# Seven products for eight in the up product of a fused retention and tanh-shrink kernel

## The chip, the cores and the metric

The kernel runs on one core of one Trainium2 chip. The metric is the device time of one execution in microseconds. Five engines work side by side, each in the order of its own queue, and wait for one another by semaphores: TensorE (PE in the profile, its weight loads PEld), VectorE (DVE), ScalarE (ACT), GpSimd (POOL) and SyncE (SP, which starts transfers). TensorE writes its results into PSUM[...]; GpSimd does not reach PSUM in this kernel.

## The reference

```python
# q, k, v: (4, 8, 768, 64)
for t in range(768):
    state = gamma * state + outer(k[t], v[t])      # per batch and head
    y[t] = scale * q[t] @ state
x = y.transpose(0, 2, 1, 3).reshape(3072, 512)
h = x @ w_in                                       # 512 -> 2048
g = h - tanh(h)
out = g @ w_out                                    # 2048 -> 512
```

All of it is in float32; `w_in` and `w_out` arrive as 64-bit floats and are converted on the chip.

## The kernel before

The tokens are cut into 24 chunks of 128 for the attention and into 12 half blocks `n` of 256 tokens (`TH`) for the two large products. The hidden dimension is cut into 8 pairs `m2` of two 128-wide tiles. A *step* is one half block with one pair, so there are 96 steps, numbered `s` from 0; half blocks 4 to 11 have eight steps each, 32 to 95.

The first steps are issued in an order written out by hand, with the conversion of the weights in between (`keep_busy` there puts filler products of 128 columns on zeros into TensorE's queue). From step 8 on one loop issues everything; each engine keeps the order of the program, since the schedule is manual. Per step the loop does this:

- `up` (line 420): 8 products, 128x128 weights of `w_in` against 256 tokens, into one PSUM bank `h` (two such banks in turn; the left and the right half hold the two tiles of the pair). Each float32 product is two instructions of TensorE, so a step has 16.
- `shrink_begin` (lines 429, 430): ScalarE takes the square `u` and the tanh `th` of the bank.
- `shrink_factors` (437 to 439): ScalarE makes `q0`, `q1` and `large` from `u`.
- `shrink_multiply` (445 to 448): VectorE makes h - tanh(h) and multiplies two factors of a polynomial onto `h`, in PSUM.
- `shrink_end` (454 to 459): the last factor, the product with `u` into `g` in SBUF, and a predicated copy that puts h - tanh(h) where |h| is not small.
- `fast_sums` (545 to 548): four sums of quarters of `g` by GpSimd, each 128x128.
- `downs(LAG)`: the down product of the step two before (`LAG` = 2).

The down product of half blocks 5 to 11 (`FAST` = 5) is already in seven products for eight, in Winograd's form of Strassen's scheme: `fast_down` (line 581) makes seven products of 256 columns (14 instructions) from sums of `g` and of `w_out`, accumulated over the eight steps of a half block in seven halves of PSUM banks. `fast_end` joins them at the end of a half block: one ScalarE copy and seven VectorE sums (lines 590 to 602), with the two output transfers on SP. `fast_weights` (line 536) makes the sums of `w_out` once, on GpSimd. For half blocks before that, `down` (line 468) makes four products of 512 columns (8 instructions).

The attention of the last chunks runs in the same loop, at odd steps up to 45: `keep_x`, `products`, `mask`, `state`, `turn_by_dma` (ScalarE copies of 16-bit words and a transfer that transposes them) and `outputs`; GpSimd scales q and v of a later chunk (`scale`, line 240) at the end of the step before.

Of the kernel before, what the change touches and what calls it, by code (L numbers as in the profile page):

```python
# [9 lines left out]
F32 = mybir.dt.float32  # L10
# [3 lines left out]
AF = mybir.ActivationFunctionType  # L14
ALU = mybir.AluOpType

P = 128
# [15 lines left out]
def kernel(  # L33
# [7 lines left out]
    tables: bass.AP,  # L41
    out: bass.AP,
):

# [11 lines left out]
    nc = tc.nc  # L58
# [10 lines left out]
    NB = NCH // BLK  # L69
    BANK = 512  # L70
    TH = 2 * P
    LAG = 2
# [3 lines left out]
    stage = ctx.enter_context(tc.tile_pool(name="stage", bufs=2))  # L76
# [20 lines left out]
    at = [0]  # L97
# [22 lines left out]
    NW = 2 * NM  # L120
# [289 lines left out]
    def work(tag, bufs):  # L410
        return tmp.tile([P, BANK], F32, tag=tag, name=tag, bufs=bufs)

    def up(n, m2, i):

        if i == 0:
            hps[n, m2] = bank("h", f"h_{n}_{m2}")
        hp = hps[n, m2][:, ts(i, TH)]
        keep_busy(hp[:, :P])
        for c in range(NC):
            nc.tensor.matmul(hp, w1[:, c, ts(2 * m2 + i, P)], xT[n // 2][:, c, ts(n % 2, TH)],  # L420
                             start=(i == 0 and c == 0), stop=(c == NC - 1),
                             skip_group_check=True)
# [3 lines left out]
    def shrink_begin(n, m2):  # L426
        hp = hps[n, m2]
        u, th = (work(x, 2) for x in ("u", "th"))
        nc.scalar.activation(u, hp, AF.Square)  # L429
        nc.scalar.activation(th, hp, AF.Tanh)  # L430
        shrinking[n, m2] = [u, th]

    def shrink_factors(n, m2):
        u = shrinking[n, m2][0]
        large = work("large", 2)
        q0, q1 = (work(x, 1) for x in ("q0", "q1"))
        nc.scalar.activation(q0, u, AF.Square, bias=bias0)  # L437
        nc.scalar.activation(q1, u, AF.Square, bias=bias1, scale=math.sqrt(A))  # L438
        nc.scalar.activation(large, u, AF.Relu, bias=bias_m)  # L439
        shrinking[n, m2] += [q0, q1, large]  # L440

    def shrink_multiply(n, m2):
        hp = hps[n, m2]
        u, th, q0 = shrinking[n, m2][:3]
        nc.vector.tensor_tensor(th, hp, th, op=ALU.subtract)  # L445
        nc.vector.scalar_tensor_tensor(hp, in0=u, scalar=R, in1=hp, op0=ALU.subtract,  # L446
                                       op1=ALU.mult, reverse0=True)
        nc.vector.scalar_tensor_tensor(hp, in0=q0, scalar=C0, in1=hp, op0=ALU.add,  # L448
                                       op1=ALU.mult)

    def shrink_end(n, m2):
        hp = hps.pop((n, m2))
        u, th, _, q1, large = shrinking.pop((n, m2))
        nc.vector.scalar_tensor_tensor(hp, in0=q1, scalar=A * C1, in1=hp, op0=ALU.add,  # L454
                                       op1=ALU.mult)
        g = gp.tile([P, 2, TH], F32, tag="g", name=f"g_{n}_{m2}")
        flat = g.rearrange("p i t -> p (i t)")
        nc.vector.tensor_tensor(flat, hp, u, op=ALU.mult)  # L458
        nc.vector.copy_predicated(flat, large.bitcast(I32), th)  # L459
        gT[n, m2] = g  # L460
# [25 lines left out]
    def rows_of(n):  # L486

        return out[ds(n * TH, TH)].rearrange("(p two) c -> p two c", two=2)
# [19 lines left out]

    FAST = 5
    PAIRS = NM // 2  # L510
    room = []
    t_of = {}

    def quarter(i, c, at):
        return w2[:, i::2, ts(c, TH)][:, ds(2 * at, 2)]

    def fast_weights(k, at):

        if not room:
            for _ in range(3):  # L520
                raw = stage.tile([P, 2, 2, TH], F32, tag="raw", name="fast_raw", bufs=3)
                room.extend(raw[:, i] for i in range(2))
            for tag in ("head", "low", "power"):
                room.extend(stage.tile([P, 2, TH], F32, tag=tag, name=f"fast_{tag}")
                            for _ in range(2))
        if k == 3 and at == 0:
            late = xp.tile([P, 4, 2, TH], F32, tag="xT", name="fast_x")
            room.extend(late[:, i] for i in range(4))
        t = t_of[k, at] = room[PAIRS // 2 * k + at]
        a, b = (  # L530
            (quarter(0, 1, at), quarter(0, 0, at)),
            (quarter(1, 1, at), t_of.get((0, at))),
            (quarter(1, 1, at), quarter(0, 1, at)),
            (t_of.get((1, at)), quarter(1, 0, at)),
        )[k]
        nc.gpsimd.tensor_tensor(t, a, b, op=ALU.subtract)

    fast_g = {}

# [28 lines left out]
        right = {2: 1, 7: 1, 4: 1, 6: n % 2}  # L568
        accs[n] = {k: b[:, ts(right.get(k, 0), TH)] for k, b in acc.items()}

    def fast_down(n, m2, first, last):
        if first:
            fast_banks(n)
        left = fast_g.pop((n, m2))
        for k in (1, 2, 4, 6, 7, 5, 3):
            right = (
                w2[:, 2 * m2, :TH], w2[:, 2 * m2 + 1, :TH], w2[:, 2 * m2 + 1, TH:],
                *(t_of[x, m2 // 2][:, m2 % 2] for x in (3, 0, 1, 2)),
            )[k - 1]

            nc.tensor.matmul(accs[n][k], left[k - 1], right, start=first and k in (1, 6, 7, 4),  # L581
                             stop=last, skip_group_check=True)

    def fast_end(n):
        acc = accs.pop(n)
        o = op.tile([P, 2, DM], F32, tag="sum", name=f"sum_{n}")
        c11, c12, c21, c22 = (o[:, j, ts(c, TH)] for j in range(2) for c in range(2))
        some = [mid.tile([P, 2, TH], F32, tag="a", name=f"fast_{n}") for _ in range(2)]
        p1, v_, x_, w_ = (t[:, i] for t in some for i in range(2))
        nc.scalar.copy(out=p1, in_=acc[1])  # L590
        add, sub = ALU.add, ALU.subtract
        for dst, k, b, how in (
            (c11, 2, p1, add), (v_, 6, p1, add), (w_, 7, v_, add), (c22, 5, w_, add),
            (x_, 5, v_, add), (c21, 4, w_, sub), (c12, 3, x_, add),
        ):
            if how is sub:
                nc.vector.tensor_tensor(dst, b, acc[k], op=sub)
            else:
                nc.vector.tensor_tensor(dst, acc[k], b, op=add)
            if dst is c21:  # L600
                nc.sync.dma_start(out=rows_of(n)[:, 1], in_=o[:, 1])
        nc.sync.dma_start(out=rows_of(n)[:, 0], in_=o[:, 0])

    waiting = []

    def part(j, n, m2, first, last):
        down(n, m2, j, first, last)
        if last:
            add_up(n, m2, j)

    def downs(lag):
        while len(waiting) > lag:
            tile_ = waiting.pop(0)
            if tile_[0] >= FAST:
                fast_down(*tile_)
                if tile_[3]:
                    fast_end(tile_[0])
                continue
            for j in range(2):
                part(j, *tile_)  # L620

# [52 lines left out]


    FIRST = 8
    LAST_WEIGHTS = NW - 6
    with_chunk = {BEGUN + 2 * i + 1: FIRST - 3 + i for i in range(NCH - FIRST + 3)}  # L680
    with_weights = {BEGUN: [12, 13]}
    for i in range(14, NW):
        with_weights[i - 5] = [i]
    fast_parts = [(k, at) for at in range(PAIRS // 2) for k in range(3)]
    fast_parts += [(3, at) for at in range(PAIRS // 2)]

    for s in range(BEGUN, len(steps)):
        n, m2, first, last = steps[s]
        ci = with_chunk.get(s)
        if ci is not None:  # L690
            if ci >= FIRST:
                outputs_rest(ci)
                keep_x(ci)
            if FIRST <= ci + 2 < NCH:
                products(ci + 2)
                mask(ci + 2)
                state(ci + 2)
            load_chunk(ci + 4)
            if ci + 3 < NCH:
                turn_by_dma(ci + 3)  # L700
            if FIRST <= ci + 1 < NCH - 1:
                outputs(ci + 1)
                see(ci + 1)
        for i in with_weights.get(s, []):
            convert(i)
            load_weights(i + 3)
        for i in range(2):
            up(n, m2, i)
        if ci == NCH - 2:
            outputs(ci + 1)  # L710
            see(ci + 1)
        waiting.append(steps[s])
        shrink_begin(n, m2)
        shrink_factors(n, m2)
        shrink_multiply(n, m2)
        downs(LAG)
        shrink_end(n, m2)
        if n >= FAST:
            fast_sums(n, m2)
        if s + 1 in with_chunk:  # L720
            for which in range(2):
                scale(with_chunk[s + 1] + 3, which, nc.gpsimd)
        if s > LAST_WEIGHTS + 1:
            for _ in range(min(2, len(fast_parts))):
                fast_weights(*fast_parts.pop(0))
    downs(0)


def _tables(H, D, S=768):
# [51 lines left out]
```

## Time and profile before

| what | us |
|---|---|
| median of 3 runs | 733.02 (732.61 to 735.18) |
| the profiled execution | 733.69 |
| its span in the profile | 731.9 |
| busy in it: TensorE, VectorE, ScalarE, GpSimd | 717.7, 533.6, 389.7, 247.6 |
| step 32 begins about | 287.7 |
| step 95 begins its up product | 713.2 |

A line of the profile's groups gives the line of the kernel, the engine, the operation, the output and inputs by name, their shapes, and the count. A line of the order in time gives the start, the length, the engine, the line, and in brackets how long the engine had been idle and what released it. The stretches give busy time and count for each engine, in the order PE, PEld, DVE, ACT, POOL, and then the granted TensorE clock, the share of the transfers and GB/s.

### The profile page before, as it was taken

What the parts mean: (1) busy time and instruction counts of PE and PEld (TensorE: products, weight loads), DVE (VectorE), ACT (ScalarE), POOL (GpSimd) and SP (SyncE); (2) the same over time, 40 slices, a digit from 0 to 9 for tenths busy, and PEclk for the clock granted to TensorE, in tenths of its full rate; (3) what the DMA queues carried; (4) which work ended last, traced back from release to release, by engine and by line L of the source; (5) the groups of instructions that cost most, each with busy time, mean ns of one, the idle gap of its engine ahead of it and who ended that gap; (6) DMA issues with size and microseconds to landing.
All of it is one profiled execution on the core that took longest, in us unless ns stands there. A gap on an engine that the chain in (4) does not pass through costs nothing.

```text
span 731.9 us, 14885 instructions
## 1 busy us (share of the span) xinstructions
PE 717.7 (98%) x5806; PEld 566.9 (77%) x5806; DVE 533.6 (73%) x849; ACT 389.7 (53%) x749; POOL 247.6 (34%) x348
## 2 busy tenths in 40 slices
PE   8899999999999999999999999999999999999996
PEld 7686666666776676677688888888888888888885
DVE  4999988998888777765566676676766766766764
ACT  4567557766777645565445444444444444444441
POOL 0565434544554555411012222222132222222221
PEclk9999999999999999999999999999999999999998
DMA  9883428776776566444100000000000000000000
GB/s 202 211 207 84 130 69 218 173 197 171 188 192 165 110 147 165 131 106 122 36 30 1 1 29 2 1 29 1 29 1 1 30 0 1 30 0 1 30 0 30
DMA packets 125399, 59.84 MB, mean 82 GB/s; under 512 B 109840, under 2 KB 118160, under 8 KB 125328
## 3 DMA queue, kind: packets, MB, share of 16 engines
q1 hardware_dynamic: 122880, 50.34, 28.4%
q10 hardware_dynamic: 2448, 8.54, 3.1%
q8 instruction: 46, 0.75, 0.4%
q14 instruction: 25, 0.20, 0.1%
HBM read 35.80 MB, written 14.68 MB: 69 GB/s over the span
## 4 chain that ended last, share of the span: by engine, by line
PE 91%; DMA 4%; DVE 2%; POOL 1%; SPq 1%; ACT 1%; issue 0%; DVEq 0%; POOLq 0%; ACTq 0%
PE h L420 44%; PE o L468 17%; PE fast_t L581 8%; PE y L581 8%; PE fast_o L581 7%; PE y L356 3%; DMA kqT<-rows 1%; PE s L302 1%; PE s L308 1%; DMA raws<-in_moe_w_in_dram 1%; DMA k<-in_k_dram 1%; DMA q<-in_q_dram 1%; SPq L233 1%; PE kqTp L254 1%; DMA rows<-apart 1%; DVE head L189 0%
## 5 line engine op out<-in xcount | busy, mean ns | idle before, releaser
L420 PE MATMUL h<-xT,w 128*128 128x256 f32 x1536 | 349.9, 381 | 1.1 <-DVE w L203 1.1
L420 PEld LDWEIGHTS h<-xT,w 128*128 128x128 f32 x1536 | 289.7, 190 | 50.1 <-issue 10.0
L429 ACT ACTIVATE u<-h 128x512 f32<-128x512 f32 x96 | 57.3, 597 | 259.7 <-PE h L420 259.5
L445 DVE TENSOR_TENSOR th<-h,th 128x512 f32<-128x512 f32 x96 | 66.2, 689 | 132.3 <-ACT th L430 132.2
L468 PE MATMUL o<-w,g 128*128 128x512 f32 x320 | 144.2, 593 | 0.0
L545 POOL TENSOR_TENSOR s<-g 128x128 f32<-128x128 f32 x56 | 25.5, 455 | 286.7 <-DVE g L459 282.3
L468 PEld LDWEIGHTS o<-w,g 128*128 128x128 f32 x320 | 60.5, 190 | 59.5 <-issue 56.7
L459 DVE COPY_PREDICATED g<-large,th 128x512 f32<-128x512 int32 x96 | 74.3, 774 | 9.8 <-DVE g L458 0.5
L448 DVE SCALAR_TENSOR_TENSOR h<-q,h 128x512 f32<-128x512 f32 x96 | 66.8, 696 | 10.0
L199 POOL TENSOR_TENSOR low<-low,power 128x512 f32<-128x512 f32 x30 | 38.6, 1288 | 102.4 <-DVE power L191 62.8
L454 DVE SCALAR_TENSOR_TENSOR h<-q,h 128x512 f32<-128x512 f32 x96 | 66.6, 694 | 8.9 <-DVE h L448 0.9
L458 DVE TENSOR_TENSOR g<-h,u 128x512 f32<-128x512 f32 x96 | 66.4, 692 | 6.9
L437 ACT ACTIVATE q<-u,tab 128x512 f32<-128x512 f32 x96 | 69.5, 724 | 0.0
L438 ACT ACTIVATE q<-u,tab 128x512 f32<-128x512 f32 x96 | 69.1, 720 | 0.0
L439 ACT ACTIVATE large<-u,tab 128x512 f32<-128x512 f32 x96 | 68.8, 716 | 0.0
L446 DVE SCALAR_TENSOR_TENSOR h<-u,h 128x512 f32<-128x512 f32 x96 | 65.8, 685 | 0.0
L430 ACT ACTIVATE th<-h 128x512 f32<-128x512 f32 x96 | 56.8, 591 | 0.0
L240 POOL TENSOR_TENSOR q<-q,tab 128x512 f32<-128x512 f32 x22 | 24.2, 1099 | 77.2 <-DMA q<-in_q_dram 52.0
L203 POOL TENSOR_TENSOR w<-low,head 128x512 f32<-128x512 f32 x30 | 38.5, 1284 | 2.4
L240 POOL TENSOR_TENSOR v<-v,tab 128x512 f32<-128x512 f32 x22 | 28.2, 1284 | 3.3 <-DMA v<-in_v_dram 3.3
L356 PEld LDWEIGHTS y<-a,v 64*64 64x64 f32 x768 | 15.9, 134 | 14.9 <-ACT large L439 10.9
L546 POOL TENSOR_TENSOR s<-s,g 128x128 f32<-128x128 f32 x56 | 25.6, 457 | 4.4
(110 smaller groups left out, 868.7 us busy)
## 6 DMA issues: line engine op xcount, KB each, us to landing
rows<-apart ACTq DMA_DIRECT2D x16, 512.0 KB, 4.4
k<-in_k_dram SPq DMA_DIRECT2D x24, 256.0 KB, 4.7
q<-in_q_dram SPq DMA_DIRECT2D x24, 256.0 KB, 5.1
v<-in_v_dram SPq DMA_DIRECT2D x24, 256.0 KB, 5.5
raw<-in_moe_w_out_dram SPq DMA_DIRECT2D x12, 512.0 KB, 4.1
out_dram<-sum SPq DMA_DIRECT2D x24, 256.0 KB, 2.3
raw<-in_moe_w_in_dram SPq DMA_DIRECT2D x14, 256.0 KB, 4.4
raw<-in_moe_w_in_dram SPq DMA_DIRECT2D x28, 128.0 KB, 4.2
```

The lines of the kernel that those rows point to most:

```text
L420: nc.tensor.matmul(hp, w1[:, c, ts(2 * m2 + i, P)], xT[n // 2][:, c, ts(n % 2, TH)], start=(i == 0 and c == 0), stop=(c == NC - 1), skip_g ...
L437: nc.scalar.activation(q0, u, AF.Square, bias=bias0)
L438: nc.scalar.activation(q1, u, AF.Square, bias=bias1, scale=math.sqrt(A))
L439: nc.scalar.activation(large, u, AF.Relu, bias=bias_m)
L445: nc.vector.tensor_tensor(th, hp, th, op=ALU.subtract)
L446: nc.vector.scalar_tensor_tensor(hp, in0=u, scalar=R, in1=hp, op0=ALU.subtract, op1=ALU.mult, reverse0=True)
L448: nc.vector.scalar_tensor_tensor(hp, in0=q0, scalar=C0, in1=hp, op0=ALU.add, op1=ALU.mult)
L454: nc.vector.scalar_tensor_tensor(hp, in0=q1, scalar=A * C1, in1=hp, op0=ALU.add, op1=ALU.mult)
L458: nc.vector.tensor_tensor(flat, hp, u, op=ALU.mult)
L459: nc.vector.copy_predicated(flat, large.bitcast(I32), th)
L468: nc.tensor.matmul(o_p[j], gT[n, m2][:, i, ts(j, P)], w2[:, 2 * m2 + i], start=(first and i == 0), stop=(last and i == 1))
L581: nc.tensor.matmul(accs[n][k], left[k - 1], right, start=first and k in (1, 6, 7, 4), stop=last, skip_group_check=True)
```

## The change

The up product of half blocks 4 to 11 (`FAST_UP` = 4, 64 steps) is put into the seven-product form too. Left are quarters of `w_in` for the pair (each two tiles of 128 deep), right are quarters of the half block's 256 tokens, 128 columns each. A step has 14 products of 128 columns (28 instructions), all into one bank of four 128-column places:

1. `fast_up(..., (1, 5, 7, 6))` makes products 1, 5, 7 and 6 in places 0 to 3.
2. `up_take`: ScalarE copies the whole bank to SBUF (one buffer, `odd_room[0]`).
3. `up_pairs`: GpSimd makes two sums from the copy, 1 + 6 and 5 + 7 (128x256, into `odd_room[1]`).
4. `fast_up(..., (2, 3, 4))` adds products 2, 3 and 4 on top of places 0, 1 and 2.
5. `up_add`: VectorE adds the first sum to places 1 and 2 (128x256) and writes the total of the two sums to place 3 (128x128).

The sums of the operands are made by GpSimd: `up_weights` once per pair, at steps 28 to 35 (four differences or sums of 128x256), `up_tokens` once per half block (four of 128x256). `fast_weights` is now made per pair, at steps 40 to 47, in other buffers and with the same number of elements.

The order within a step changes as well. The factors of a step are split over two: the loop first ends the step before (`shrink_factors`, `shrink_end`), then does `up_pairs`, the sums for later steps, `fast_sums` of the step before, up to two of the output sums that `fast_end` now leaves for later (`end_some(2)`), the first half of the down product, the second products, `up_add`, tanh and square of `h` (tanh first), `q0`, the second half of the down product, and two factors. The last two steps have an order of their own.

```diff
     def shrink_begin(n, m2):
         hp = hps[n, m2]
         u, th = (work(x, 2) for x in ("u", "th"))
-        nc.scalar.activation(u, hp, AF.Square)
-        nc.scalar.activation(th, hp, AF.Tanh)
+        if n < FAST_UP:
+            nc.scalar.activation(u, hp, AF.Square)
+            nc.scalar.activation(th, hp, AF.Tanh)
+        else:
+            nc.scalar.activation(th, hp, AF.Tanh)
+            nc.scalar.activation(u, hp, AF.Square)
         shrinking[n, m2] = [u, th]
+
+    def shrink_factor(n, m2):
+        q0 = work("q0", 1)
+        nc.scalar.activation(q0, shrinking[n, m2][0], AF.Square, bias=bias0)
+        shrinking[n, m2].append(q0)
...
+    PLACE = {1: 0, 5: 1, 7: 2, 6: 3, 2: 0, 3: 1, 4: 2}
+
+    def fast_up(n, m2, some):
+        if 1 in some:
+            hps[n, m2] = bank("h", f"h_{n}_{m2}")
+        for k in some:
+            for c in range(2):
+                nc.tensor.matmul(hps[n, m2][:, ts(PLACE[k], P)], s_of[m2][k - 1][:, c],
+                                 x_of[n][k - 1][:, c], start=(k == 1 and c == 0), stop=(c == 1),
+                                 skip_group_check=True)
+
+    def up_take(n, m2):
+        nc.scalar.copy(out=odd_room[0], in_=hps[n, m2])
+
+    def up_pairs():
+
+        first = odd_room[0].rearrange("p (i t) -> p i t", i=4)
+        nc.gpsimd.tensor_tensor(odd_room[1], first[:, :2], first[:, 3:1:-1], op=ALU.add)
+
+    def up_add(n, m2):
+        hp = hps[n, m2].rearrange("p (i t) -> p i t", i=4)
+        u, w = (odd_room[1][:, i] for i in range(2))
+        nc.vector.tensor_tensor(hp[:, 1:3], hp[:, 1:3],
+                                u[:, None, :].to_broadcast([P, 2, P]), op=ALU.add)
+        nc.vector.tensor_tensor(hp[:, 3], u, w, op=ALU.add)
...
+    def up_weights(m2):
+
+        a11, a12, a21, a22 = (w1[:, ds(2 * c, 2), ts(2 * m2 + i, P)]
+                              for i in range(2) for c in range(2))
+        s_ = {k: next(up_room).rearrange("p (c m) -> p c m", c=2) for k in (2, 3, 4)}
+        s_[1] = a21
+        for k, x, y, how in ((3, a11, a21, ALU.subtract), (1, a21, a22, ALU.add),
+                             (2, s_[1], a11, ALU.subtract), (4, a12, s_[2], ALU.subtract)):
+            nc.gpsimd.tensor_tensor(s_[k], x, y, op=how)
+        s_of[m2] = (a11, a12, s_[4], a22, s_[1], s_[2], s_[3])
+
+    def up_tokens(n, t):
+
+        x = xT[n // 2][:, :, ts(n % 2, TH)]
+        b11, b12, b21, b22 = (x[:, ds(2 * c, 2), ts(i, P)] for c in range(2) for i in range(2))
+        t = t.rearrange("p (k c t) -> p k c t", k=4, c=2)
+        t1, t2, t3, t4 = (t[:, i] for i in range(4))
+        for dst, a, b in ((t1, b12, b11), (t2, b22, t1), (t3, b22, b12), (t4, b21, t2)):
+            nc.gpsimd.tensor_tensor(dst, a, b, op=ALU.subtract)
+        x_of[n] = (b11, b21, b22, t4, t1, t2, t3)
+
...
+    def end_some(n):
+        for _ in range(min(n, len(ending))):
+            ending.pop(0)()
...
         nc.scalar.copy(out=p1, in_=acc[1])
+        add(c11, 2, p1)
+        add(v_, 6, p1)
+        for args in ((w_, 7, v_), (c22, 5, w_), (x_, 5, v_), (c21, 4, w_, True), (c12, 3, x_)):
+            ending.append(lambda args=args: add(*args))
...
+        if fast:
+            fast_up(n, m2, (1, 5, 7, 6))
+            up_take(n, m2)
+        else:
+            for i in range(2):
+                up(n, m2, i)
         if ci == NCH - 2:
             outputs(ci + 1)
             see(ci + 1)
         waiting.append(steps[s])
-        shrink_begin(n, m2)
-        shrink_factors(n, m2)
-        shrink_multiply(n, m2)
-        downs(LAG)
-        shrink_end(n, m2)
-        if n >= FAST:
-            fast_sums(n, m2)
+        if fast:
+
+
+            final = s == len(steps) - 1
+            if final:
+                shrink_factor(*before)
+                shrink_multiply(*before)
+            if before:
+                shrink_factors(*before)
+                if final:
+                    shrink_last_factor(*before)
+                else:
+                    shrink_end(*before)
+            up_pairs()
+            for make in with_sums.get(s, []):
+                make()
+            if before and before[0] >= FAST and not final:
+                fast_sums(*before)
+            end_some(2)
+            downs(LAG, int(final))
+            fast_up(n, m2, (2, 3, 4))
+            up_add(n, m2)
+            shrink_begin(n, m2)
+            if final:
+                shrink_end(*before, begun=True)
+                fast_sums(*before)
+            if s != len(steps) - 2:
+                shrink_factor(n, m2)
+                if not final:
+                    downs(LAG, 1)
+                shrink_multiply(n, m2)
+            before = n, m2
+        else:
+            shrink_begin(n, m2)
+            shrink_factors(n, m2)
+            shrink_multiply(n, m2)
+            downs(LAG)
+            shrink_end(n, m2)
+            for make in with_sums.get(s, []):
+                make()
         if s + 1 in with_chunk:
             for which in range(2):
                 scale(with_chunk[s + 1] + 3, which, nc.gpsimd)
-        if s > LAST_WEIGHTS + 1:
-            for _ in range(min(2, len(fast_parts))):
-                fast_weights(*fast_parts.pop(0))
+    shrink_factors(*before)
+    shrink_end(*before)
+    fast_sums(*before)
     downs(0)
+    end_some(len(ending))
```

## The prediction

> **What bounds the kernel now.** I read the engine totals first, then the chain of work that ended last, then the stage that the change touches by stretches, then one step of it in order of time.
>
> ```profile
> PE 717.7 (98%) x5806; PEld 566.9 (77%) x5806; DVE 533.6 (73%) x849; ACT 389.7 (53%) x749; POOL 247.6 (34%) x348
> PE h L420 44%; PE o L468 17%; PE fast_t L581 8%; PE y L581 8%; PE fast_o L581 7%; PE y L356 3%; DMA kqT<-rows 1%; PE s L302 1%; PE s L308 1%; DMA raws<-in_moe_w_in_dram 1%; DMA k<-in_k_dram 1%; DMA q<-in_q_dram 1%; SPq L233 1%; PE kqTp L254
> ```
>
> TensorE carries the span, and the up product (L420) is 44% of the chain. The stretches (busy us and count for PE, PEld, DVE, ACT, POOL) show the last 50 steps, 389.4 to 713.2 us: no hole in TensorE, VectorE at 68%. The chain there has one period: 16 up instructions, then 14 down instructions.
>
> ```profile
> 389.40:713.20 323.80, 323.80 (x1503) 285.05 (x1502) 219.60 (x342) 147.76 (x258) 87.10 (x200) 1.00 0.03 11
> 603.29 3.45 PE h L420 x16
> 608.47 1.29 PE y L581 x6
> 609.76 3.45 PE h L420 x16
> ```
>
> So a step takes 609.76 - 603.29 = 6.47 us: 16 x 0.2157 = 3.45 up and 14 x 0.2157 = 3.02 down. One step of the other engines, in order of time:
>
> ```profile
> 561.45 0.60 ACT L429 ACTIVATE u<-h 128x512 f32<-128x512 f32 x1 [3.56 <-PE h L420]
> 561.95 0.59 ACT L430 ACTIVATE th<-h 128x512 f32<-128x512 f32 x1
> 562.57 0.69 DVE L445 TENSOR_TENSOR th<-h,th 128x512 f32<-128x512 f32 x1 [1.94 <-ACT th L430]
> 563.18 0.69 DVE L446 SCALAR_TENSOR_TENSOR h<-u,h 128x512 f32<-128x512 f32 x1
> 563.97 0.70 DVE L448 SCALAR_TENSOR_TENSOR h<-q,h 128x512 f32<-128x512 f32 x1
> 564.77 0.70 DVE L454 SCALAR_TENSOR_TENSOR h<-q,h 128x512 f32<-128x512 f32 x1
> 565.57 0.69 DVE L458 TENSOR_TENSOR g<-h,u 128x512 f32<-128x512 f32 x1
> 566.36 0.74 DVE L459 COPY_PREDICATED g<-large,th 128x512 f32<-128x512 int32 x1
> 567.24 0.45 POOL L545 TENSOR_TENSOR s<-g 128x128 f32<-128x128 f32 x1 [4.65 <-DVE g L459]
> ```
>
> VectorE's six instructions need 3.79 us from the first start to the last start, plus 0.74; a dependent one starts 0.80 after its forerunner, an independent one 0.61. Its idle 1.94 us is the whole reserve that the change may use, and part of that is the time for ScalarE's two reads of h.
>
> [...] in the step above VectorE reads h only after both of ScalarE's reads. [...] the predicated copy, 0.74 us alone, took 1.50 when it met a GpSimd difference and ended 0.61 after that.
>
> ```profile
> 289.96 1.27 POOL L536 TENSOR_TENSOR fast_head<-w,fast_raw 128x512 f32<-128x512 f32 x1
> 290.34 1.50 DVE L459 COPY_PREDICATED g<-large,th 128x512 f32<-128x512 int32 x1
> ```
>
> **TensorE.** The up product of a step becomes 14 products of 128 columns instead of 8 of 256, each two instructions: 28 for 16. The price of 128 columns is in the opening filler:
>
> ```profile
> 30.92 2.08 PEld L216 LDWEIGHTS kqTp<-busy 128*128 128x128 f32 x18 [1.94 <-issue]
> 30.95 2.25 PE L216 MATMUL kqTp<-busy 128*128 128x128 f32 x18 [1.83 <-DVE state L331]
> ```
>
> Less one duration (0.19, 0.275) that is 1.89/17 = 0.111 and 1.98/17 = 0.116 us from start to start; I take 0.1115. 28 x 0.1115 = 3.12 against 3.45: 0.33 saved, a step of 6.14. [...]
>
> **VectorE, the step that decides.** The new order per step is: last factor, g and predicated copy of the step before; up to two deferred output sums; two sums into h (up_add); then th and two factors of this step. Start to start:
> - th to the predicated copy's start, unchanged: 3.79.
> - The copy to the first sum: 0.74 less the overlap of independent ones (0.69 - 0.61): 0.66.
> - The first sum, 128x256 out of PSUM: 0.34 to the next, as 725.89 to 726.23 in the closing output sums (below). The second, 128x128: full tiles take 0.69, half tiles 0.416, so a quarter 0.28.
> - Handing over to ScalarE isn't shown; VectorE to GpSimd is 0.14 (567.10 to 567.24). Bounds 0 and 0.14; I take 0.10.
> - ScalarE's tanh and square of h: 1.09 (561.45 to 562.54), and 0.03 to th. The change puts tanh first, so th could start after 0.59, but both instructions read the same bank[...]. Bounds 0.62 and 1.12; I take 1.12.
>
> Sum 3.79 + 0.66 + 0.34 + 0.28 + 0.10 + 1.12 = **6.29**, already above 6.14. The second sum has both inputs in SBUF, while GpSimd starts fast_sums 0.14 after the copy (0.46 each): it would start at 0.26 and may wait until 0.60. Bounds 0 and 0.34, I take 0.10: 6.39. Per eight steps there are more: five deferred sums at 0.36 (1.8); in one step fast_end's two sums stand ahead of th and wait for ScalarE's copy p1, which is queued behind the third activation (tanh's start + 0.50 + 0.47 + 0.62 + 0.37 = 1.96, then 0.03 and two spacings of 0.34: th at 2.67 instead of 1.12: 1.55); one predicated copy meets the token differences (0.7 in most blocks, so 0.5). 3.85/8 = 0.48. **6.87 a step.**
>
> ```profile
> 725.89 0.42 DVE L599 TENSOR_TENSOR sum<-y,fast 128x256 f32<-128x256 f32 x1 [3.39 <-ACT fast L590]
> 726.23 0.41 DVE L599 TENSOR_TENSOR fast<-fast_o,fast 128x256 f32<-128x256 f32 x1
> ```
>
> TensorE then waits: the copy of h by ScalarE comes after the third activation of the step before, and the second products wait for that copy; behind them stand the second half of the down product and the next step's first products.
>
> **What is hidden.** The copy itself (0.6, priced as L429) lies under the first half of the down product (8 x 0.2157 = 1.73); without that cover it would cost 0.7 per step. ScalarE, 46% busy, rises by 0.6 us a step. GpSimd: a sum of 128x256 is some 0.73 (between 0.457 for 128 columns and 1.27 for 512); per step 0.73 + 1.83 for fast_sums, and 2.9 more where weights or tokens are combined: 5.5, under the step. Before step 40 the weight sums also stand ahead of the chunk scaling for which ScalarE's word copies wait: 0 to 0.5 us in six steps; I take 0. SP's two output transfers per half block move later by one or two steps with nothing queued behind them that is waited for: 0.
>
> **Sum.** Steps 32 to 41 share TensorE with the attention: two steps take 16.05 us (312.63 to 328.68), VectorE 6.29 + 0.75 (mask and states) + up to 0.7 stays below 7.7, so TensorE keeps the end: 10 x -0.33 = -3.3. Steps 42 to 45 (7.0 each now) about +1. Steps 46 to 94: 49 x (6.87 - 6.475) = +19.4. The end, where the last two tiles' factors lie open behind the sums: 0 to +2, I take +0.7. Together +17.8. The profiled execution took 733.69 us (span 731.9 and 1.8 around it), 0.7 above the median of 733.02: 733.0 + 17.8, about **750 us**, 2.3% slower.
>
> **Rivals.**
> - *th starts at tanh's end* (no hold[...]). Each step 0.5 less: 5.79 + 0.10, so most steps fall back to TensorE's 6.14 and only the four with extra work exceed it: 6.34 to 6.58 on average. 49 x (-0.135 to +0.10) - 3 + 0.7 gives -9 to +3: about 728. For it: tanh was put first. [...]
> - *TensorE stays the bound throughout*, should the sums and handovers be far cheaper and the deferred work fit the gaps: 6.14. 49 x -0.33 - 5 + 0.7 = -20: 713. It decides the sign as soon as VectorE's mean falls under 6.45. Against it: 6.29 is made of measured spacings.
> - *Weight loads don't overlap*: 28 x 0.190 = 5.32 up, 8.34 a step, 62 x 1.87 = +116: 849. The filler's 0.111 speaks against it.
>
> That the sums are wrong products is not a rival: left and right operands make the four blocks.
>
> **Chances.** Forecast 0.58, mostly slower, 0.03 of it within the bound; first rival 0.27 (0.14 faster, 0.11 within, 0.02 slower); second 0.12; third 0.03. Within 0.5% is what a measurement of this kernel can tell from no change. Faster 0.26, same 0.14, slower 0.60. The forecast's own range is 740 to 766 (bank hold fixed[...], 0 to 0.14 handover); with the rivals 718 to 766, which leaves out part of the second and the third.
>
> **What would show it.** Right: 28 up instructions 0.11 us apart; VectorE idle about 1.1 us ahead of th at each step and never idle ahead of up_add; TensorE waiting ahead of the second products; steps of 6.4 us and one of 8 in eight. Wrong: VectorE waiting for TensorE ahead of up_add, th starting 0.6 us after tanh, steps of 6.14.

## The result and the profile after

The changed kernel took **803.23 us** (median of four, 801.98 to 805.48) against 733.12 for the kernel before on the same chip: **1.095 times as long, 95% interval 1.092 to 1.099**. The prediction said 750, at most 766. The 70 us are four times the predicted 17.8.

I read the result in the same order as the kernel before. First the engine totals, the TensorE clock by slices, and the chain that ended last:

```profile
PE 728.4 (91%) x6574; PEld 587.2 (73%) x6574; DVE 581.3 (73%) x977; ACT 430.5 (54%) x813; POOL 350.2 (44%) x492
...
PEclk9999999999999999999998998899889999999799
...
PE 57%; DVE 27%; ACT 8%; issue 5%; POOL 2%; DVEq 0%; ACTq 0%; POOLq 0%
```

Three things have changed. TensorE is busy for 91% of the span instead of 98%, so it has holes. The slices are 20 us long, and the clock falls below 9 tenths only from about 420 us on, in groups. And VectorE, which had 2% of the chain before, now has 27% of it. No engine is the bound: TensorE and VectorE take turns. Where an engine at 73% carries a quarter of the chain, look for two engines that wait for each other.

The stretches (busy us and count of PE, PEld, DVE, ACT, POOL, then granted clock, share of the transfers and GB/s) show that the loss is not in every step. Two stretches of about one half block, of 56 and 62 us:

```profile
611.00:667.00 56.00, 52.52 (x347) 46.58 (x347) 42.15 (x74) 28.80 (x50) 23.30 (x44) 1.00 0.03 10
549.00:611.00 62.00, 49.98 (x299) 44.99 (x299) 37.13 (x64) 25.69 (x45) 21.12 (x40) 0.89 0.03 9
```

From the first `th` (L445 before, L455 after) of a half block to the first of the next, the eight steps took, in us:

| half block | before | after |
|---|---|---|
| 4 | 64.0 | 66.3 |
| 5 | 57.1 | 57.3 |
| 6 | 51.8 | 64.1 |
| 7 | 51.8 | 71.9 |
| 8 | 51.8 | 67.9 |
| 9 | 51.8 | 55.1 |
| 10 | 51.8 | 54.8 |

Half blocks 9 and 10 need 55.0, which is 6.87 us a step, **exactly the step that was predicted**. Half blocks 6 to 8 need up to 17 more. The first steps of half block 11 need 9.1 more (8.13, 11.97 and 11.42 us, where those of half block 9 take 8.12, 7.30 and 6.98).

TensorE's waits from 405 to 780 us (us in total, times, longest) say what is special there. The same stretch of the kernel before has no entry.

```profile
PE fast_t L609 <- DVE sum L627: 17.5, 4, 6.6
PE y L609 <- DVE sum L627: 11.9, 3, 6.6
PE y L609 <- DVE sum L625: 6.6, 1, 6.6
PE fast_t L609 <- DVE fast L627: 6.2, 2, 3.1
PE fast_t L609 <- DVE sum L625: 4.3, 1, 4.3
PE h L681 <- ACT fast_head L686: 4.2, 7, 1.1
```

The first five rows are 46.5 us: the down product of a *new* half block waits for the output sums of the *old* one. All but two waits of 1.1 us are for sums that `fast_end` has left for later. The last row is the wait that the prediction had expected ahead of the second products. It is small.

One of those holes, where half block 7 goes over into 8, VectorE and TensorE in order of time (in brackets the idle time before an instruction and what ended it):

```profile
572.14 0.69 DVE L473 TENSOR_TENSOR g<-h,u 128x512 f32<-128x512 f32 x1
572.93 0.73 DVE L474 COPY_PREDICATED g<-large,th 128x512 f32<-128x512 int32 x1
...
573.88 0.41 DVE L625 TENSOR_TENSOR sum<-fast,y 128x256 f32<-128x256 f32 x1
...
574.35 2.08 PE L609 MATMUL y<-w,g 128*128 128x256 f32 x4 [6.61 <-DVE sum L625]
...
580.29 0.43 DVE L696 TENSOR_TENSOR h<-h,fast_head 128x256 f32<-128x256 f32 x1 [6.00 <-PE h L681]
```

TensorE stands for 6.61 us until one output sum of 0.41 us has ended, because that sum is queued on VectorE behind the whole round of the step before (g, predicated copy). Then VectorE stands for 6.00 us, because its next instruction, `up_add`, needs the second products, which stand on TensorE behind the down product that had just been released. Each engine's queue puts the thing that the other needs last: lock-step.

### The profile page after: what moved, and what is told of

Its sections match the earlier page's. It is cut to its first block, busy times and chain, and to the rows that moved or that the text cites. A ratio compares the mean times of both kernels' runs of the same rounds, so it can differ in the third digit from the quotient of the medians.

```text
span 801.6 us, 16809 instructions
## 1 busy us (share of the span) xinstructions
PE 728.4 (91%) x6574; PEld 587.2 (73%) x6574; DVE 581.3 (73%) x977; ACT 430.5 (54%) x813; POOL 350.2 (44%) x492
## 4 chain that ended last, share of the span: by engine, by line
PE 57%; DVE 27%; ACT 8%; issue 5%; POOL 2%; DVEq 0%; ACTq 0%; POOLq 0%
PE o L483 15%; PE h L421 13%; PE h L681 12%; DVE g L473 4%; DVE h L463 4%; PE fast_t L609 4%; PE y L609 3%; DVE h L458 3%; ACT th L434 3%; DVE th L455 3%; PE y L357 3%; PE fast_o L609 3%; DVE h L456 3%; ACT u L435 2%; DVE h L696 2%
## 5 line engine op out<-in xcount | busy, mean ns | idle before, releaser
L434 ACT ACTIVATE th<-h 128x512 f32<-128x512 f32 x64 | 38.2, 597 | 242.7 <-DVE h L698 230.1
L483 PE MATMUL o<-w,g 128*128 128x512 f32 x320 | 146.0, 594 | 0.0
L455 DVE TENSOR_TENSOR th<-h,th 128x512 f32<-128x512 f32 x96 | 66.2, 689 | 81.1 <-ACT u L435 67.3
L691 POOL TENSOR_TENSOR fast_head<-fast_head 128x256 f32<-128x256 f32 x64 | 47.2, 738 | 174.8 <-ACT fast_head L686 174.8
L421 PE MATMUL h<-xT,w 128*128 128x256 f32 x512 | 117.7, 382 | 1.2 <-DVE w L204 1.2
L421 PEld LDWEIGHTS h<-xT,w 128*128 128x128 f32 x512 | 95.7, 190 | 21.1 <-issue 7.2
L681 PEld LDWEIGHTS h<-xT,w 128*128 128x128 f32 x512 | 78.6, 200 | 28.2 <-ACT fast_head L686 12.9
L681 PE MATMUL h<-xT,w 128*128 128x128 f32 x512 | 84.7, 290 | 5.3 <-ACT fast_head L686 4.2
L474 DVE COPY_PREDICATED g<-large,th 128x512 f32<-128x512 int32 x96 | 76.4, 795 | 9.9
L681 PE MATMUL h<-x,w 128*128 128x128 f32 x448 | 69.9, 280 | 0.0
L473 DVE TENSOR_TENSOR g<-h,u 128x512 f32<-128x512 f32 x96 | 66.3, 691 | 3.3
L696 DVE TENSOR_TENSOR h<-h,fast_head 128x256 f32<-128x256 f32 x64 | 27.8, 434 | 47.6 <-PE h L681 47.5
L681 PEld LDWEIGHTS h<-x,w 128*128 128x128 f32 x448 | 60.7, 197 | 0.0
```

What stands on the lines that cost most here:

```text
L483: nc.tensor.matmul(o_p[j], gT[n, m2][:, i, ts(j, P)], w2[:, 2 * m2 + i], start=(first and i == 0), stop=(last and i == 1))
L681: nc.tensor.matmul(hps[n, m2][:, ts(PLACE[k], P)], s_of[m2][k - 1][:, c], x_of[n][k - 1][:, c], start=(k == 1 and c == 0), stop=(c == 1), ...
```

## The experiments

All were timed with the kernel before on the same chip (733.5 to 733.7 us); ratios are to that, with 95% intervals.

**The deferred sums made at once.** In `fast_end`:

```diff
-            ending.append(lambda args=args: add(*args))
+            add(*args)
```

> The changed kernel, but fast_end makes all seven output sums at once again, so nothing is left for later steps. Theory T (TensorE's first down products of a half block are ordered against the deferred sums of the half block before, because their banks lie in one two-bank tensor): the holes of up to 6.6 us in TensorE at the half block boundaries go, 48 us less, a little back for five sums that stand in one step: 755 us (745 to 762). Rival V (VectorE is simply late at the boundaries, and the same sums are on it at any order): 790 us or more.

Measured: 761.97 us, ratio 1.040 (1.037 to 1.042), 41 us less than the change, and above the forecast of 755 but inside its range. Most of the hole time is gone and half blocks 6 to 10 take 55.0 to 57.7; the longest holes left are 4.22 and 4.30 us, at 6 to 7 and 7 to 8. So most of the loss hangs on the deferral. This doesn't yet say whether the sums' time or the banks that they read matter.

**The same deferral, but the accumulators kept apart.** The seven half-bank accumulators (a `bank` of the kernel is 512 float32 columns on 128 partitions, as `h` in the traces) lie in two two-bank tensors (`fast_t`, and `y`, which was the attention's) and in two single banks (`fast_o`). The rotation in `fast_banks` moves through them so that a new half block never gets a bank that the deferred sums still read, but often *the other bank of its tensor*. The edit lets the halves that the deferred sums read (products 3, 4, 5 and 7) change between the two tensors and keeps the others in fixed banks:

```diff
-            spare.append([t[:, 0], t[:, 1], o[0], whole[:, 0], whole[:, 1]])
+            spare.append([(t[:, 0], t[:, 1]), (whole[:, 0], whole[:, 1])])
+            spare.append(o[0])
             spare.append(o[1])
-        five, sixth = spare
-        first, second, third = five[:3]
-        spare[0] = five[3:] + [first, second, third]
+        first, sixth = spare[1:]
+        second, third = spare[0][(n - FAST) % 2]
```

> The changed kernel with the sums still deferred, but the accumulators are dealt out otherwise: products 1 and 2 always in the single bank fast_o, products 3, 4, 5 and 7 in turn in the two banks of fast_t and the two banks of y, so that no half block uses a tensor from which the half block before still has deferred sums. T: every half block takes what the undisturbed ones took (54.9 us, 6.87 a step), 755 us (745 to 760), no hole over 2 us. Rival V: holes stay, 790 us or more.

Measured: 756.18 us, ratio 1.031 (1.029 to 1.033), **47.0 less than the change**, with the same instructions of the engines in the same order, on other banks. Half blocks 6 to 10 now take 54.8 to 55.2. TensorE's waits shrink to short ones, on the sums that `fast_end` doesn't defer and on the copy of `h`:

```profile
PE fast_o L609 <- DVE sum L627: 11.1, 6, 2.0
PE h L681 <- ACT fast_head L686: 6.0, 16, 0.6
```

**The deferral alone, put into the kernel before.** The edit of `fast_end` and `end_some` as in the change, and in the loop:

```diff
         shrink_multiply(n, m2)
+        end_some(2)
         downs(LAG)
```

> The kernel before with the deferral alone: fast_end makes two sums, the other five follow two per step. VectorE is 68% busy here. T: holes of 3 us or more in TensorE at the boundaries 5 to 6, 6 to 7, 7 to 8 and 10 to 11, none at 8 to 9 and 9 to 10; 755 to 775 us. Rival V (holes need a VectorE that is full): within 3 us of the kernel before.

Measured: 778.14 us (two runs), ratio 1.061 (1.058 to 1.064), 3 over the top of the range. The 44 us come without any of the new up products. VectorE and TensorE in one of its holes:

```profile
500.44 0.41 DVE L595 TENSOR_TENSOR sum<-fast,fast_t 128x256 f32<-128x256 f32 x1
...
500.90 2.07 PE L581 MATMUL fast_t<-w,g 128*128 128x256 f32 x4 [3.96 <-DVE sum L595]
...
511.68 0.69 DVE L445 TENSOR_TENSOR th<-h,th 128x512 f32<-128x512 f32 x1 [8.59 <-ACT th L430]
```

The holes lie where half block 5 goes over into 6, 6 into 7, 7 into 8 and 10 into 11, and nowhere else: just the four places where the rotation gives old sums and new products a common tensor. At 8 to 9 and 9 to 10 it gives them none.

**The deferral in the kernel before, with the accumulators apart** (the edits of the last two together).

> The kernel before with the deferral and the banks dealt out apart. T: the deferral itself costs nothing, 733 us within 2 us, no hole at the boundaries. Rival (late sums hold TensorE in any bank): 760 us or more.

Measured: 732.93 us (ten runs), ratio 0.9998 (0.9987 to 1.0009), no holes. Against the 778.14 of the last experiment, the deferral costs nothing by itself; deferral and rotation together cost 45 us. This settles the cause for the kernel before as the second experiment does for the change.

**No sums into h**: the second experiment without the calls of `up_take`, `up_pairs` and `up_add`, so that `h` stays incomplete.

> The second one of this call (banks apart), leaving out the ScalarE copy of h, GpSimd's pair sums and VectorE's two sums into h; the output is then not the reference's. Theory D (the step is set by VectorE's round of six instructions, two sums and the wait for tanh and square): steps fall from 6.43 to TensorE's 6.14, 720 to 730 us. Rival P (128-column products with their waits set the step): steps stay at 6.4, within 6 us of the second one.

Measured: 711.43 us (two runs), ratio 0.970 (0.968 to 0.972), lower than the 720 to 730 expected. The stretch of steps:

```profile
409.00:700.00 291.00, 291.00 (x1985) 273.80 (x1984) 209.67 (x329) 146.69 (x246) 94.19 (x207) 1.00 0.03 12
```

TensorE has no hole and a step takes 6.15 us, the 6.14 that 28 x 0.1115 + 3.02 had given. So the saving on TensorE is real, 22 us; the copy, GpSimd's sums and VectorE's two sums together take 45 from there to 756.

**Square before tanh**, in the second experiment's kernel:

```diff
-            nc.scalar.activation(th, hp, AF.Tanh)
             nc.scalar.activation(u, hp, AF.Square)
+            nc.scalar.activation(th, hp, AF.Tanh)
```

> Banks apart, with ScalarE's square ahead of tanh as in the kernel before. Hold (th waits for both reads of the bank whatever their order): same time within 2 us of the banks-apart run, 756 us. Rival (th is released by tanh alone): 0.5 us a step more, about 780 us.

Measured: 753.94 us, ratio 1.028 (1.026 to 1.029), against 756.18. That is 2.2 less, just past the 2 expected, and far from the rival's 780. Putting tanh first gained nothing. With tanh first, `th` started 1.12 us after the tanh's start, when the square had ended too (601.05 and 602.17 in the change, shown below); in the kernel before, with the square first, 1.12 after the square's start, when the tanh had ended too (561.45 and 562.57).

**The predicated copy moved behind the sums.** If VectorE's round is too long because it stands idle for 1.2 us ahead of `th`, other work can be put there. On the second experiment's kernel, `shrink_end` leaves its predicated copy for later; the loop does it behind `up_add`, `tanh` and `square`, and then `fast_sums`; `fast_end`'s ScalarE copy goes ahead of the activations, its two sums to the same place.

```diff
                 else:
-                    shrink_end(*before)
+                    copy_rest = shrink_end(*before, later=True)
...
-            if before and before[0] >= FAST and not final:
-                fast_sums(*before)
-            end_some(2)
...
             downs(LAG, int(final))
             fast_up(n, m2, (2, 3, 4))
+            sums_now = fast_end(ended) if ended else None
             up_add(n, m2)
             shrink_begin(n, m2)
+            if before and not final:
+                copy_rest()
+                if before[0] >= FAST:
+                    fast_sums(*before)
+            if ended:
+                sums_now()
+            else:
+                end_some(2)
```

> Banks apart, and VectorE's order changed: the predicated copy of the step before and the deferred output sums stand behind the two sums into h, in the time in which ScalarE makes tanh and square; fast_end's copy p1 stands ahead of tanh and its two sums in the same place. D (VectorE's round with its idle 1.2 us sets the step): the round falls from 6.39 to about 5.5, TensorE becomes the bound, steps of 6.15 throughout, 714 us (711 to 722), faster than the kernel before. Rival C (ScalarE's chain tanh, square, q0, copy of h sets it): steps stay at 6.3 or more, 725 us or more.

Measured: **718.01 us** (717.62 to 719.17), ratio 0.979 (0.978 to 0.981): faster than both kernels. One step of VectorE and ScalarE:

```profile
604.03 0.43 DVE L706 TENSOR_TENSOR h<-h,fast_head 128x256 f32<-128x256 f32 x1
...
604.50 0.30 DVE L708 TENSOR_TENSOR h<-fast_head 128x128 f32<-128x128 f32 x1
604.71 0.74 DVE L477 COPY_PREDICATED g<-large,th 128x512 f32<-128x512 int32 x1
...
604.89 0.60 ACT L434 ACTIVATE th<-h 128x512 f32<-128x512 f32 x1 [2.05 <-DVE h L708]
...
606.01 0.69 DVE L455 TENSOR_TENSOR th<-h,th 128x512 f32<-128x512 f32 x1 [0.56 <-ACT u L435]
```

The copy of 0.74 now lies inside the wait for ScalarE, of which 0.56 is left. VectorE's round falls below TensorE's 6.15 and TensorE is the bound again (98% busy).

**The copy behind, `fast_end` left where it was** behind the third activation.

> As the first of this call, but fast_end stays behind the third activation. D: steps of 6.15, except that at each of the six half block boundaries the step with fast_end's wait is 1 to 2.5 us longer: 6 to 14 us more than the first. Rival C: as far above 725 us as the first.

Measured: 723.60 us, ratio 0.986 (0.985 to 0.988), 5.6 more than with `fast_end` moved, just under the 6 to 14 expected. From one predicated copy to the next, one step per half block takes 7.11 us and the following one 5.95, a net 0.76 a half block. So the predicated copy, with `fast_sums` and the deferred sums that moved behind it, carries 32.6 of the 38 us between 756 and 718, and `fast_end`'s place the rest. What the copy alone is worth was not tried.

**The fastest version with the rotation of the change.**

> The kernel with the copy behind the sums (718 us), but with the rotation of accumulator banks of the changed kernel. T: the holes come back at four boundaries, as long as VectorE's path from the deferred sum back to TensorE, which is shorter here than in the changed kernel: 20 to 40 us more, 738 to 758 us. Rival (sharing hurts only while VectorE is the bound): within 5 us of 718 us.

Measured: 736.39 us, ratio 1.004 (1.001 to 1.007), 18.4 more than with the accumulators apart, a little below the 20 to 40 expected. TensorE's waits:

```profile
PE fast_t L615 <- DVE sum L633: 7.0, 4, 2.0
PE y L615 <- DVE sum L633: 3.5, 2, 2.0
```

With the order mended, the shared tensors still eat all that the seven products bring. The waits stand at three boundaries. Why there is none at 7 to 8 can be read from the order of this loop. The output sums stand here between the two halves of the down product (products 1, 2, 4 and 6, then 7, 5 and 3). At the three boundaries each wait is one of the second half, right behind the sums: once the old half block's product 7, 1.96 us for `fast_end`'s first sum, and twice the new one's product 3, for deferred sums. At 7 to 8 only products 1 and 2 lie on the tensor that the deferred sums read, and they come ahead of each step's sums; the old product 7 lies on another tensor than the one that `fast_end`'s first sum reads.

## Why the prediction was wrong

**The step that failed** is the pricing of the deferral. The prediction counted it as VectorE's time alone ("five deferred sums at 0.36 (1.8)") and SP's ("SP's two output transfers per half block move later by one or two steps with nothing queued behind them that is waited for: 0"). It went past what the moved sums *hold*: as long as they have not run, the accumulators that they read are taken, here with the other bank of the same tensor, and the next user of that bank is TensorE's down product of the new half block. None of the rivals contained that. Its size by the half blocks of the change is what they have above 55.0, 9.1 + 16.9 + 12.9, and 9.1 at the start of half block 11: 48.0. By experiment it is 803.2 - 756.2 = 47.0 (on two chips, on which the kernel before differed by 0.5).

Which accumulators wait could have been worked out beforehand. Call the two banks of `fast_t` t0 and t1, those of `y` w0 and w1, and the single bank in the rotation o0. For products 1, 2 / 5, 7 / 3, 4, the rotation gives half block 5 the banks t0, t1, o0, half block 6 w0, w1, t0, half block 7 t1, o0, w0, half block 8 w1, t0, t1, half block 9 o0, w0, w1. The deferred sums read the last two of each three. At 7 to 8 they read o0 and w0 while the new products write w1, t0 and t1: no common *bank*, but w0 and w1 are one *tensor*. The same holds at 5 to 6, 6 to 7 and 10 to 11. The runs show that instructions on different banks of one tensor waited for each other here (up to 6.61 us in the change and 3.96 with the deferral in the kernel before), and that with the deferred sums on other tensors they don't: in the kernel before TensorE is then busy for all of the 291 us from 409 to 700, and in the change its longest wait from 405 to 745 us is 2.0, for sums that aren't deferred. The profile names VectorE's sums from events of semaphores, so the waits are in the program; whether the chip would need them was not tried.

**TensorE's term** was right. Sixteen first instructions of a step, then the down product:

```profile
606.97 0.61 PE L681 MATMUL h<-xT,w 128*128 128x128 f32 x4
...
608.75 1.03 PE L609 MATMUL y<-w,g 128*128 128x256 f32 x4
```

(608.75 - 606.97) / 16 = 0.111 us, against 0.1115 taken; the step of 6.15 without the sums into h bears out 6.14. The rival in which weight loads don't overlap is refuted.

**VectorE's round** was right. An ordinary step took 6.43, predicted 6.39. That `th` is held for the square as well as the tanh was an assumption of the prediction; the trace shows it. Of the 48 steps whose `th` starts between 404.6 and 776.4 us, 42 have VectorE stand ahead of it until the square has ended, 50.9 us in all, 1.21 each; in the other six the sums of `fast_end` stand there. So the rival in which `th` starts at tanh's end is refuted, and with it the one in which TensorE stays the bound:

```profile
600.57 0.40 DVE L698 TENSOR_TENSOR h<-fast_head 128x128 f32<-128x128 f32 x1
...
601.05 0.60 ACT L434 ACTIVATE th<-h 128x512 f32<-128x512 f32 x1 [2.52 <-PE fast_t L609]
...
601.55 0.59 ACT L435 ACTIVATE u<-h 128x512 f32<-128x512 f32 x1
...
602.17 0.69 DVE L455 TENSOR_TENSOR th<-h,th 128x512 f32<-128x512 f32 x1 [1.21 <-ACT u L435]
```

VectorE is idle for 1.21 until the square has ended, not the tanh; whether the program or the chip asks for that was not tried. The handover from VectorE to ScalarE is 601.05 - (600.57 + 0.40) = 0.08 (0.10 taken). The second sum took 0.40, while GpSimd's first sum of `fast_sums` ran (600.35 to 600.80); it took 0.30 at 604.50 in the fastest version, where GpSimd was idle from 602.51 to 605.59. So the 0.10 that the prediction had estimated for GpSimd was the right size there; the 42 from 450 to 780 us took 0.30 to 0.58, 0.37 on average.

**The extras** were right in the sum: one step with `fast_end` lost 1.69 (tanh at 682.20, `th` at 685.01, instead of 1.12; predicted 1.55), the deferred sums about 1.65 (7.30, 6.98 and 6.66 us for 6.43; predicted 1.8), the token sums about 0.27 (0.5). That is 3.6 in eight steps for the 3.85 predicted, and the eight ordinary steps are 0.3 longer than predicted. So the exact 6.87 is in part luck: two small errors cancel.

**The chunk stage** was a term mis-sized by about 5 us. Half block 4 was forecast some 2.6 below its 64.0 and came out 2.3 above. TensorE waits there for ScalarE's copies of the attention's output:

```profile
311.90 0.63 ACT L402 COPY xT<-y 128x256 f32<-128x256 f32 x2
...
312.58 0.69 PE L357 MATMUL y<-kqT,state 64*64 64x64 f32 x32 [1.71 <-ACT xT L402]
```

That wait came five times, 5.1 us in all. In the kernel before, it was these copies that waited for TensorE, seven times from 287 to 400 us, 5.8 us in all. The prediction let VectorE alone speak for that stage. But tanh and square moved behind `up_add`, and what stands behind them in ScalarE's queue moved too; that queue was not followed. Without the sums into h (the experiment above) half block 4 took 61.4, 2.6 less than before, as forecast, and TensorE had no such wait. So the loss hangs on the sums into h and the copy of `h` for them; which of them delays ScalarE's copies was not tried.

**The account:** 17.8 predicted, 47 for the shared tensors and about 5 in the chunk stage make 70, the measured 803.2 - 733.1.

## What to carry to other kernels

When an instruction is put off, ask not only what its own time costs where it goes, but which buffer it holds until it has run, who writes that buffer next, and how long the queue is in which it now stands: here 0.41 us of work held TensorE for up to 6.61. Work that out for each turn of a rotation, and by tensors as well as by banks, since the trouble showed in four turns of six. And where a round is too long because it contains a wait on another engine (here 1.2 us for two reads of a bank), first look for independent work in the same queue that can be put into the wait: moving the copy of 0.74 us, and the sums behind it, turned a loss of 3.1% into a gain of 1.4%, and of 2.1% with `fast_end`'s two sums moved as well.

## What the runs showed of the hardware

A hole cost TensorE more than its length here. After the 6.61 us hole the granted clock was 0.50; from 580 to 584 us it was 1.00 again, as at 604 (the third column from the end):

```profile
574.00:578.00 4.00, 3.65 (x9) 2.94 (x10) 0.29 (x1) 0.00 (x0) 1.54 (x4) 0.50 0.17 66
604.00:608.00 4.00, 4.00 (x31) 3.79 (x30) 3.49 (x6) 0.82 (x3) 3.92 (x6) 1.00 0.00 0
```

Four instructions of 256 columns took 2.08 us at 574.35, against the 1.03 at 608.75 above. The twenty instructions from there to 580.02 took 5.67 us; at the 0.2157 and 0.1115 apiece of the prediction they would have taken 3.06. So, as an estimate, about 2.6 of the 6.00 us for which VectorE then waited are TensorE's slower clock. The slow stretch lasted from 574.35 to about 579.5, some 5.2 us.

The length of the hole alone doesn't tell whether the clock falls. Behind a hole of 3.08 us in the change (443.09) it was 0.50, and two instructions of 256 columns took 1.22. Behind one of 3.63 (deferral in the kernel before, 576.99) it was 1.00, and the next two took 0.59. Behind the three of 1.12 and 1.13 in the change (561.84, 629.76 and 684.82) it was 1.00 as well. What sets it was not shown. The mean clock of the change was 0.966, against 0.989 with the accumulators apart and 0.996 in the fastest version.
